# Decode attention on Trainium2: K's words sorted by pairs of heads, dense exponentials, and a mask on the transposed probabilities

## The chip, the cores and the metric

The kernel runs on one core of one Trainium2 chip. The metric is the device time of one execution in microseconds. Three runs of the kernel before took 481.1, 480.31 and 480.0 us; their median is 480.31 us. A profile of one further execution goes with them.

## The reference, cut to what matters

One decode step of a transformer layer for a batch of B = 4 sequences with one new token each, model width D = 576. All inputs are bf16.

```
q = layernorm(x) @ wq                       # 32 query heads of 128
k, v = the last 4096 positions of the caches  # 16 KV heads, 2 query heads on each
p = softmax(q . k / sqrt(128))              # per query head, over 4096 positions
h = x + (p . v) @ wo
out = h + (relu(g) * u) @ W_down            # g, u = layernorm(h) @ W_gate, W_up
```

The caches have 16384 positions, of which the last 4096 are read: 67 MB of K and 67 MB of V. The weights add 25 MB.

## The kernel before, in words

All programs are written out by hand, one per engine. `Sched` (line 51) turns names into semaphore waits: an operation lists the names it depends on, each engine runs its own list strictly in the order written, and all transfers are issued by SP in one list (line 270), each waiting until its place in the SBUF tile `pool` is free.

**Quads and batches.** The 64 pairs of a sequence and a KV head are worked on four heads at a time. A quad is one sequence's four KV heads: 4 MB of K and 4 MB of V. There are 16 quads, and two of them form a batch; there are eight batches, n = 0 to 7. `pool` has four slots of one quad each. In the queue a K quad is followed by the V quad of two quads before, and each waits for the earlier user of its slot: K for its transposes (`("TR", 2i+1)`), V for its matmuls (`("PV", i)`). The weights of the output projection and of the MLP come behind, in the same places.

**Layout of K.** A quad lies in SBUF with partition 4p+s holding head s of 32 position groups p (128 positions t per partition). VectorE transposes it in 32x32 blocks of 4-byte words (`tr`, line 403): a word is two neighbouring features e = 0, 1, and 64 words c, k make a position. One transpose instruction does a quarter of a quad, 2048 words per partition. After it the partition is the word of the feature and the 32 columns of a block are the 32 source partitions, eight position groups k by four heads s. Before the change the output pattern sorts these by head: all columns of head 0, then of head 1 and so on, so that the next written word is 1024 words (4 KB) on. Two instructions fill one of the two buffers of `kT`, which is one block f of the work; there are 32 blocks, four per batch.

**QK** (`qk`, line 540). A block takes 16 matmuls: four heads s by four parts (c, e) of the feature. Each moves 512 columns (64 t by 8 k) through weights `qz`, which are q with zeros elsewhere, and all add into one PSUM bank. The words of a head are contiguous, but of each word a matmul reads one half, so the moving operand has a step of 4 bytes. Row 32g+8r+2s+h of the scores is position group quadrant g, quad r of the batch, head s, query h.

**Softmax** (`rmax`, `fbias`, `trp`, from line 414). Per batch VectorE takes the row maximum, GpSimd makes it common to all rows of a head (`partition_all_reduce`, line 298), and VectorE forms the bias. A V quad lies in SBUF as a K quad does, so after transposing the probabilities partition 4p+s meets head s of V, and there the probabilities of other heads must be zero. Before the change ScalarE makes that so (line 348): it takes the exponential of each score bank four times, u = 0 to 3, with a bias that is about -1.5e38 on rows of other heads than u, and writes copy u to every fourth place of `P`, 8 bytes apart. Two transposes per batch (line 431) then turn `P` into `pT`, 2048 elements per partition each.

**PV** (`pv`, line 556). 32 matmuls per quad move V (512 columns) through weights of 32 columns of `pT`.

**Orders around the change.** TensorE (line 580): blocks 2i and 2i+1 of QK, then PV of quad i-2; so within a batch: QK, QK, PV, QK, QK, PV. At three places `ext` (line 569) stands in front of a PV; it takes finished outputs out. VectorE (line 445): the four transposes of quad 2n, those of quad 2n+1, then `rmax`, `fbias`, `trp` and the row sums of batch n; `norm` (line 439) stands at three places between the two quads and waits for `ext`. A transpose of block f waits until QK of block f-2 has read its buffer. ScalarE: the copies of q into `qz` (`qzero`, line 315), then the batch's exponentials, which wait for the bias, and before the change for the transposes of P of the batch before, since `P` has one buffer.

**Ends.** Before the first batch the layer norm, the q projection (line 523) and its copies (449, 450) run while the first K quad lands. After the last batch come its two PVs, `ext`, `norm`, a shuffle of the outputs (465, 469), the output projection (line 594), the second layer norm and the MLP; W_gate is released by the first of the last PVs, W_up by the second, W_down by the end of the output projection.

Of the kernel before, what the change touches and what calls it, by code (L numbers as in the profile page):

```python
# [6 lines left out]
ACT = mybir.ActivationFunctionType  # L7
ALU = mybir.AluOpType
# [14 lines left out]
NS = 4  # L23
# [80 lines left out]
def bass_sequential_preLN__sliding_block_cached__glu_gated_reglu__decode_kernel(  # L104
# [12 lines left out]
    with ExitStack() as es:  # L117
# [26 lines left out]
        mask = sb("mask", [128, 3, NHB], FP32)  # L144
        selT = sb("selT", [128, 4, H], FP32)
        rmx = sb("rmx", [128, 2], FP32)
        rsel = sb("rsel", [128, NS], FP32)
        bmin = sb("bmin", [128, 2], FP32)
        pmax = sb("pmax", [128, 2, NHB], FP32)
        bcm = sb("bcm", [128, 2, NHB], FP32)  # L150
        t8 = sb("t8", [128, NHB], FP32)
        bias = sb("bias", [128, 2, NS], FP32)
        rs2 = sb("rs2", [128, 2, 2 * NS], FP32)
# [14 lines left out]
        hh = P[:, NG * JW:NG * JW + NG * JW // 2].bitcast(BF16).rearrange("p (g j f) -> p g j f", g=NG, j=JJ)  # L168
        hhT = probT[:, 0, 0:FC * 16].bitcast(BF16).rearrange("p (f b) -> p f b", b=32)
        S8 = probT[:, 0, FC * 16:FC * 16 + 512].bitcast(BF16)  # L170
        Pb = P[:, :].bitcast(BF16).rearrange("p (x s) -> p x s", s=NS)
        Pw = P[:, :].bitcast(BF16)
        x_f = P[0:B, 0:D]
        junk_f = P[0:B, D:2 * D]
        pT = [probT[:, a, :].bitcast(BF16).rearrange("p (a t h) -> p t a h", t=TQ, h=NHQ) for a in range(2)]
# [126 lines left out]
        def prog_act(S):  # L302
            a = "scalar"
            S.dma(a, lambda e: e.dma_start(out=x_bf[:, :], in_=A_x.rearrange("b s d -> (b s) d")), "x", name=land("x"))
            S.op(a, lambda e: e.activation(out=x_f[:, :], in_=x_bf[:, :], func=ACT.Identity, accum_out=st1[:, 0:1]),
                 deps=[land("x")], name="A_SUM")
            S.op(a, lambda e: e.activation(out=junk_f[:, :], in_=x_bf[:, :], func=ACT.Square, accum_out=st1[:, 1:2]),
                 name="A_SQ")
            S.op(a, lambda e: e.activation(out=st1[:, 4:5], in_=st1[:, 3:4], func=ACT.Sqrt, bias=eps_c[0:B, 0:1], scale=1.0),
                 deps=["D_VARC", "EPS"], name="A_STD")  # L310
            S.op(a, lambda e: e.activation(out=xn_bf[:, :], in_=x_f[:, :], func=ACT.Identity,  # L311
                                           bias=st1[:, 6:7], scale=st1[:, 5:6]),
                 deps=["D_NMR", "A_SUM"], name="A_XN")
# [13 lines left out]

            def cpy(b):
                deps = [("PV", NPB * b + NPB - 1)]
                if b >= 2:  # L330
                    deps.append(("EXT", b - 2))
                S.op(a, lambda e: e.copy(out=cp[:, b % 2, :], in_=pb[PVB + b % 2]), deps=deps, name=("CP", b))  # L332

            for i in range(NB):
                qzero(i)
            for n in range(NBATCH):
                for i in range(NB * (n + 1), min(NB * (n + 2), NQUAD)):
                    qzero(i)
                for th in range(2):
                    for u in range(NS):  # L340
                        deps = []
                        if th == 0 and u == 0:
                            deps = [("BIAS", n)]
                            if n >= 1:
                                deps.append(("TRP", n - 1, 1))
                            if n >= 2:
                                deps.append(("RSUM", n - 2))
                        S.op(a, lambda e, n=n, th=th, u=u: e.activation(  # L348
                            out=Pb[:, th * 512:(th + 1) * 512, u], in_=pb[2 * (n % 2) + th], func=ACT.Exp,
                            scale=SCALE, bias=bias[:, n % 2, u:u + 1], accum_out=rs2[:, n % 2, NS * th + u:NS * th + u + 1]),  # L350
                            deps=deps, name=("EXP", n, th) if u == NS - 1 else None, signal=u == NS - 1)
                if n >= 2 and n % 2 == 0:
                    cpy(n // 2 - 1)
            cpy(B - 1)
            S.op(a, lambda e: e.activation(out=st2[:, 24:28], in_=st2[:, 20:24], func=ACT.Sqrt),
                 deps=["D_VARC2"], name="A_STD2")
            for x in PARTS[2:] + PARTS[:2]:
                S.op(a, lambda e, x=x: e.activation(out=gate_sb[:, x[0], :, x[1]:x[2]].rearrange("p j f -> p f j"), in_=part(0, x, "f j"), func=ACT.Relu),
                     deps=[("GATE", x[3])], name=("RELU", x[0], x[1]))
            S.op(a, lambda e: e.copy(out=out_sb[:, 0:HD], in_=pb[DNB][0:B, 0:HD]), deps=["DOWN1"], name="OUT0")  # L360


        def prog_dve(S):
# [24 lines left out]
            for u in range(NS):  # L388
                S.op(v, lambda e, u=u: e.tensor_reduce(out=rsel[:, u:u + 1], in_=mask[:, 1, :].rearrange("p (r s h) -> p s r h", s=NS, h=2)[:, u, :, :],
                                                       axis=AX.XY, op=ALU.max), deps=["M1"] if u == 0 else [], name=f"RSEL{u}")  # L390
# [12 lines left out]
            def tr(i, j):  # L403
                f = 2 * i + j // 2
                deps = [land(("K", i))]
                if f >= NKH:
                    deps.append(("QK", f - NKH))
                x0 = at[("K", i)] + j * (QUAD // 4)
                src = pool[:, x0:x0 + QUAD // 4].bitcast(FP32).rearrange("p (t c k) -> p c t k", c=2, k=32)
                dst = kT[:, f % NKH, :].rearrange("p (s c t k) -> p c t k s", s=NS, c=2, k=8)[:, :, (j % 2) * (TQ // 4):(j % 2 + 1) * (TQ // 4), :, :]  # L410
                src = src.rearrange("p c t (k s) -> p c t k s", s=NS)
                S.op(v, lambda e: e.transpose(out=dst, in_=src), deps=deps, name=("TR", f) if j % 2 else None)  # L412

            def rmax(n):
# [5 lines left out]
            def fbias(n):  # L420
# [4 lines left out]
                S.op(v, lambda e: e.tensor_scalar(out=bias[:, n % 2, :], in0=rsel[:, :], scalar1=bmin[:, n % 2:n % 2 + 1], scalar2=None, op0=ALU.min),  # L425
                     deps=[("BMIN", n), f"RSEL{NS - 1}"] + ([("EXP", n - 2, 1)] if n >= 2 else []), name=("BIAS", n))

            def trp(n):
                for th in range(2):
                    h0, h1 = th * TQ // 2, (th + 1) * TQ // 2  # L430
                    S.op(v, lambda e, h0=h0, h1=h1: e.transpose(out=pT[n % 2][:, h0:h1, :, :], in_=Pw[:, h0 * 32:h1 * 32].rearrange("p (t a h) -> p t a h", a=4, h=NHQ)),  # L431
                         deps=[("EXP", n, th)] + ([("PV", NB * (n - 2) + NB - 1)] if n >= 2 and th == 0 else []), name=("TRP", n, th))
                b, q = divmod(n, 2)
                S.op(v, lambda e: e.tensor_reduce(out=rs1[:, n % 2:n % 2 + 1], in_=rs2[:, n % 2, :], axis=AX.X, op=ALU.add),  # L434
                     name=("RS1", n))
# [72 lines left out]
        def prog_pe(S):  # L508
# [31 lines left out]
            def qk(f):  # L540
                i, th = divmod(f, 2)
                n, r = divmod(i, NB)
                kv_ = kT[:, f % NKH, :].bitcast(BF16).rearrange("p (s c x e) -> p s c e x", s=NS, c=2, e=2)
                deps = [("TR", f)]
                if th == 0:
                    deps.append(("QZ", i))
# [149 lines left out]
```

## Time and profile before

| | |
|---|---|
| runs | 481.1, 480.31, 480.0 us |
| profiled execution, its own time | 481.18 us |
| its span, first to last instruction | 479.9 us |
| busy: TensorE matmul | 283.4 us (59%) |
| busy: VectorE | 301.4 us (63%) |
| busy: ScalarE | 103.8 us (22%) |
| transfers | 159.84 MB, mean 333 GB/s |
| mean granted TensorE clock | 0.839 of full |
| chain that ended last: VectorE, TensorE, ScalarE, DMA | 45%, 27%, 16%, 8% of the span |

A row of the costliest groups gives the line, the engine, the operation, out<-in by the program's names with partitions x elements and type, the count, then busy time and the mean of one in ns, then the idle time of the engine just before, with what ended most of it. All matmuls but the first transposes have line 512, that of a helper, and are told apart by their tiles: `sc<-kT,qz` is QK, `pb<-pool,probT` with 512 columns is PV. DVE is VectorE, ACT ScalarE, PE TensorE, POOL GpSimd. The chain of work that ended last lists start, duration and what ran; "issue" is time in which the engine waited for nothing that the profile shows. The timeline lists the same columns for all instructions of an engine, neighbours merged with a count.

### The profile page before, as it was taken

To read this page: it belongs to the slowest core of one execution; us is meant where nothing else is said; L and a number is where in the kernel's file an instruction comes from. 1 tells how busy PE (TensorE), PEld (TensorE's weight loads), DVE (VectorE), ACT (ScalarE), POOL (GpSimd) and SP (SyncE) were. 2 spreads that over 40 slices of the span, in tenths; PEclk is the share of its full clock that TensorE was granted. 3 is DMA by queue.
4 is the path that set the end of the run, shared out by engine and by line. 5 is a ranking of instruction groups with operands and counts; after the bars stand their busy time and mean duration, and the time that the engine had idled before them with its cause. 6 is when DMAs were issued, how large, how long until landed. Compare 5 with 4: busy or idle time off the path is not lost.

```text
span 479.9 us, 3896 instructions
## 1 busy us (share of the span) xinstructions
PE 283.4 (59%) x1669; PEld 127.4 (27%) x1684; DVE 301.4 (63%) x201; ACT 103.8 (22%) x213; POOL 8.2 (2%) x22
## 2 busy tenths in 40 slices
PE   0326702994299429690599069742894286939575
PEld 0312200341034114230243024211341142314553
DVE  0289639963996395917992778539963959140313
ACT  3010090008000800043005300080008000441002
POOL 3100000000000000000000000000000000000000
PEclk9999865898599859996799679895999599879569
DMA  8999990599859986898199948994689768926996
GB/s 347 429 436 437 436 402 8 216 393 436 355 219 393 436 352 262 350 419 369 44 385 427 421 167 350 433 393 180 262 359 438 341 262 350 384 99 237 422 409 265
DMA packets 7377, 159.84 MB, mean 333 GB/s; under 512 B 824, under 2 KB 960, under 8 KB 2112
## 3 DMA queue, kind: packets, MB, share of 16 engines
q1 hardware_dynamic: 7352, 159.59, 79.6%
q8 instruction: 13, 0.21, 0.2%
q14 instruction: 4, 0.03, 0.0%
q10 hardware_dynamic: 8, 0.00, 0.0%
HBM read 159.58 MB, written 0.00 MB: 333 GB/s over the span
## 4 chain that ended last, share of the span: by engine, by line
DVE 45%; PE 27%; ACT 16%; DMA 8%; issue 1%; SPq 1%; POOL 1%
DVE kT L412 35%; PE sc L512 17%; ACT P L348 16%; PE pb L512 10%; DMA pool<-in_A_k_cache_dram 5%; DVE probT L431 4%; DMA pool<-in_B_W_down_dram 3%; DVE rmx L415 2%; SPq L259 1%; POOL bcm L298 1%; DVE P L469 0%; DVE pmax L417 0%; DVE bias L425 0%; DVE rowsum L436 0%; DVE t L421 0%
## 5 line engine op out<-in xcount | busy, mean ns | idle before, releaser
L412 DVE STREAM_TRANSPOSE kT<-pool 128x2048 f32<-128x2048 f32 x64 | 229.3, 3704 | 3.6 <-DMA pool<-in_A_k_cache_dram 3.6
L512 PE MATMUL sc<-kT,qz 128*128 128x512 bf16 x497 | 138.0, 437 | 150.6 <-DVE kT L412 149.9
L512 PE MATMUL pb<-pool,probT 128*32 128x512 bf16 (+1 forms) x584 | 119.8, 372 | 10.9 <-DVE rs L434 7.8
L512 PEld LDWEIGHTS sc<-kT,qz 128*128 128x128 bf16 x512 | 52.0, 107 | 236.1 <-DVE kT L412 161.2
L348 ACT ACTIVATE P<-sc,bias 128x512 bf16<-128x512 f32 x64 | 77.5, 1417 | 55.7 <-DVE bias L425 55.7
L431 DVE STREAM_TRANSPOSE probT<-P 128x2048 bf16<-128x2048 bf16 x16 | 37.0, 2312 | 59.6 <-ACT P L348 59.6
L512 PEld LDWEIGHTS pb<-pool,probT 128*32 128x32 bf16 (+1 forms) x584 | 51.3, 96 | 77.6 <-issue 9.1
L325 ACT COPY qz<-qrep 32x32 bf16<-32x32 bf16 x64 | 13.9, 218 | 255.4 <-PE sc L512 244.2
L415 DVE TENSOR_REDUCE rmx<-sc 128x1 f32<-128x1024 f32 x8 | 9.8, 1224 | 35.6 <-PE sc L512 35.6
L440 DVE RECIPROCAL rs_sb<-pb 128x32 f32<-128x32 f32 x4 | 1.4, 358 | 30.7 <-PE pb L512 30.7
L348 ACT ACTIVATION_READ_ACCUMULATOR P<-sc,bias 128x1 f32 x64 | 18.8, 295 | 0.0
L519 PE MATMUL pb<-ident_b,xn_bf 4*128 4x4 bf16 (+1 forms) x5 | 0.4, 180 | 19.7 <-ACT xn_bf L311 19.7
L298 POOL PARTITION_ALL_REDUCE bcm<-pmax x8 | 3.1, 388 | 394.0 <-DVE pmax L417 394.0
L512 PE MATMUL sc<-oX,pool 128*128 128x4 bf16 (+1 forms) x160 | 6.8, 177 | 5.0 <-DVE oX L472 3.7
L373 DVE COPY sel<-ident_b 128x128 bf16<-128x128 bf16 x4 | 1.1, 450 | 11.8 <-POOL ident_b L283 11.8
L512 PEld LDWEIGHTS sc<-oX,pool 128*128 128x128 bf16 (+1 forms) x160 | 6.6, 123 | 5.4 <-issue 5.3
L332 ACT COPY cp<-pb 128x512 f32<-128x512 f32 x4 | 2.7, 673 | 17.6 <-PE pb L512 17.6
L512 PE MATMUL sc<-pool,hnT 128*32 128x288 bf16 (+2 forms) x112 | 5.8, 328 | 0.0
L499 DVE TENSOR_TENSOR P<-pb,P 128x288 bf16<-128x288 f32 (+1 forms) x2 | 0.8, 402 | 7.7 <-PE sc L512 7.7
L519 PEld LDWEIGHTS pb<-ident_b,xn_bf 4*128 4x128 bf16 (+1 forms) x5 | 0.3, 117 | 19.7 <-ACT xn_bf L311 19.7
L474 DVE TENSOR_TENSOR R_sb<-sc,xT 128x16 f32<-128x16 f32 x1 | 0.2, 174 | 8.3 <-PE sc L512 8.3
L512 PEld LDWEIGHTS pb<-selT,cp 128*128 128x128 f32 x32 | 4.1, 191 | 1.7 <-ACT cp L332 1.2
(103 smaller groups left out, 75.1 us busy)
## 6 DMA issues: line engine op xcount, KB each, us to landing
pool<-in_A_k_cache_dram SPq DMA_DIRECT2D x16, 4096.0 KB, 17.8
pool<-in_A_v_cache_dram SPq DMA_DIRECT2D x16, 4096.0 KB, 13.9
pool<-in_A_wo_dram SPq DMA_DIRECT2D x4, 1152.0 KB, 9.7
pool<-in_B_W_gate_dram SPq DMA_DIRECT2D x1, 4608.0 KB, 13.6
pool<-in_B_W_up_dram SPq DMA_DIRECT2D x1, 4608.0 KB, 20.1
pool<-in_A_wq_dram SPq DMA_DIRECT2D x1, 4096.0 KB, 13.2
pool<-in_B_W_down_dram SPq DMA_DIRECT2D x2, 1296.0 KB, 11.7
pool<-in_B_W_down_dram SPq DMA_DIRECT2D x5, 432.0 KB, 14.8
```

What stands on the lines that cost most here:

```text
L259: lambda e, g0=g0, g1=g1, j0=j0, nj=nj: e.dma_start(out=wd_sb[:, g0:g1, j0 * D:(j0 + nj) * D], in_=B_W_down[g0 * 128 * JJ:g1 * 128 * JJ, : ...
L298: S.op(g, lambda e, n=n: e.partition_all_reduce(bcm[:, n % 2, :], pmax[:, n % 2, :], 128, bass_isa.ReduceOp.max), deps=deps, name=("PAR", n))
L325: S.op(a, lambda e, src=src, dst=dst: e.copy(out=dst, in_=src), deps=deps, name=("QZ", i) if g == 3 else None, signal=g == 3)
L332: S.op(a, lambda e: e.copy(out=cp[:, b % 2, :], in_=pb[PVB + b % 2]), deps=deps, name=("CP", b))
L348: S.op(a, lambda e, n=n, th=th, u=u: e.activation(out=Pb[:, th * 512:(th + 1) * 512, u], in_=pb[2 * (n % 2) + th], func=ACT.Exp, scale=SCA ...
L373: S.op(v, lambda e, ce=ce: e.tensor_copy(out=sel[:, ce, :, :], in_=bass.AP(tensor=ident_b, offset=64 * (ce // 2) + ce % 2, ap=[[128, 128], ...
L412: S.op(v, lambda e: e.transpose(out=dst, in_=src), deps=deps, name=("TR", f) if j % 2 else None)
L415: S.op(v, lambda e: e.tensor_reduce(out=rmx[:, n % 2:n % 2 + 1], in_=sc[:, (n % 2) * 1024:(n % 2 + 1) * 1024], axis=AX.X, op=ALU.max), dep ...
L431: S.op(v, lambda e, h0=h0, h1=h1: e.transpose(out=pT[n % 2][:, h0:h1, :, :], in_=Pw[:, h0 * 32:h1 * 32].rearrange("p (t a h) -> p t a h", ...
L440: S.op(v, lambda e: e.reciprocal(out=rs_sb[:, b, :], in_=pb[OB][:, 64 + b * H:64 + (b + 1) * H]), deps=[("SUM", b)], name=("RS", b))
L499: S.op(v, lambda e, x=x: e.tensor_tensor(out=hh[:, x[0], :, x[1]:x[2]], in0=part(1, x, "j f"), in1=gate_sb[:, x[0], :, x[1]:x[2]], op=ALU. ...
L512: S.op(t, lambda e: e.matmul(o, lhsT=l, rhs=r, start=start, stop=stop, skip_group_check=skip), deps=deps, name=name, signal=name is not None)
```

## The change

It has four parts. (1) The transposes of K sort the 32 columns of a block by pairs of heads only: the output pattern runs over position group x, pair a and head within the pair s, so two neighbouring words (8 bytes) are written together, and the next two 8 KB on. (2) QK reads its head out of such a pair: the moving operand has a step of 8 bytes in runs of eight columns, 128 bytes apart. (3) ScalarE takes each exponential once, with one bias column, and writes it densely; `P` becomes double-buffered, so the exponentials wait for the transposes of two batches before. The transposes of P read each element four times over (a step of 0), which puts a copy on the partitions of all four heads. (4) VectorE then multiplies `pT` of each of the two quads by a mask `m8` (one where the partition's head is the row's, zero elsewhere), in place, 1024 elements per partition; PV waits for that product. Three small operations of the set-up are replaced by three others (`RSEL`, `M4`, `M8`).

```diff
-        rsel = sb("rsel", [128, NS], FP32)
+        rsel = sb("rsel", [128, 1], FP32)
+        m4 = sb("m4", [128, NS], FP32)
+        m8 = sb("m8", [128, NS, 2], BF16)
...
-        Pb = P[:, :].bitcast(BF16).rearrange("p (x s) -> p x s", s=NS)
-        Pw = P[:, :].bitcast(BF16)
+        Pb = P[:, :].bitcast(BF16)
...
-                    for u in range(NS):
-                        deps = []
-                        if th == 0 and u == 0:
-                            deps = [("BIAS", n)]
-                            if n >= 1:
-                                deps.append(("TRP", n - 1, 1))
-                            if n >= 2:
-                                deps.append(("RSUM", n - 2))
-                        S.op(a, lambda e, n=n, th=th, u=u: e.activation(
-                            out=Pb[:, th * 512:(th + 1) * 512, u], in_=pb[2 * (n % 2) + th], func=ACT.Exp,
-                            scale=SCALE, bias=bias[:, n % 2, u:u + 1], accum_out=rs2[:, n % 2, NS * th + u:NS * th + u + 1]),
-                            deps=deps, name=("EXP", n, th) if u == NS - 1 else None, signal=u == NS - 1)
+                    deps = []
+                    if th == 0:
+                        deps = [("BIAS", n)]
+                        if n >= 2:
+                            deps += [("TRP", n - 2, 1), ("RSUM", n - 2)]
+                    x0 = (n % 2) * 1024 + th * 512
+                    S.op(a, lambda e, n=n, th=th, x0=x0: e.activation(
+                        out=Pb[:, x0:x0 + 512], in_=pb[2 * (n % 2) + th], func=ACT.Exp,
+                        scale=SCALE, bias=bias[:, n % 2:n % 2 + 1], accum_out=rs2[:, n % 2, th:th + 1]),
+                        deps=deps, name=("EXP", n, th))
...
+            S.op(v, lambda e: e.tensor_reduce(out=rsel[:, :], in_=mask[:, 1, :], axis=AX.X, op=ALU.max), deps=["M1"], name="RSEL")
+            S.op(v, lambda e: e.tensor_reduce(out=m4[:, :], in_=ident_b[:, :].rearrange("p (b s) -> p s b", s=NS), axis=AX.X, op=ALU.add), name="M4")
+            S.op(v, lambda e: e.tensor_copy(out=m8[:, :, :], in_=bass.AP(tensor=m4, offset=0, ap=[[NS, 128], [1, NS], [0, 2]])), deps=["M4"], name="M8")
...
-                src = pool[:, x0:x0 + QUAD // 4].bitcast(FP32).rearrange("p (t c k) -> p c t k", c=2, k=32)
-                dst = kT[:, f % NKH, :].rearrange("p (s c t k) -> p c t k s", s=NS, c=2, k=8)[:, :, (j % 2) * (TQ // 4):(j % 2 + 1) * (TQ // 4), :, :]
-                src = src.rearrange("p c t (k s) -> p c t k s", s=NS)
+                src = pool[:, x0:x0 + QUAD // 4].bitcast(FP32).rearrange("p (x a s) -> p x a s", a=2, s=2)
+                dst = kT[:, f % NKH, :].rearrange("p (a x s) -> p x a s", a=2, s=2)[:, (j % 2) * TQ * 4:(j % 2 + 1) * TQ * 4, :, :]
...
-                S.op(v, lambda e: e.tensor_scalar(out=bias[:, n % 2, :], in0=rsel[:, :], scalar1=bmin[:, n % 2:n % 2 + 1], scalar2=None, op0=ALU.min),
+                S.op(v, lambda e: e.tensor_tensor(out=bias[:, n % 2:n % 2 + 1], in0=rsel[:, :], in1=bmin[:, n % 2:n % 2 + 1], op=ALU.min),
...
+                    src = bass.AP(tensor=P, offset=((n % 2) * 1024 + th * 512) // 2, ap=[[TQ * 16, 128], [1, 256]]).bitcast(BF16)
+                    src = bass.AP(tensor=src.tensor, offset=src.offset, ap=[src.ap[0], [1, 512], [0, NS]])
+                    dst = pT[n % 2][:, h0:h1, :, :]
+                    S.op(v, lambda e, src=src, dst=dst: e.transpose(out=dst, in_=src),
...
+                for a in range(NB):
+                    w = pT[n % 2][:, :, a, :]
+                    S.op(v, lambda e, w=w: e.tensor_tensor(out=w, in0=w, in1=bass.AP(tensor=m8, offset=0, ap=[[NHQ, 128], [0, TQ], [1, NHQ]]), op=ALU.mult),
+                         deps=[("TRP", n, 1)] + (["M8"] if n == 0 else []), name=("W", n, a))
...
-                kv_ = kT[:, f % NKH, :].bitcast(BF16).rearrange("p (s c x e) -> p s c e x", s=NS, c=2, e=2)
+                kv_ = kT[:, f % NKH, :].bitcast(BF16).rearrange("p (a t c k s e) -> p a s c e t k", a=2, c=2, k=8, s=2, e=2)
...
-                        mm(pb[2 * (n % 2) + th], qz[:, r, s, ce, :], kv_[:, s, ce // 2, ce % 2, :],
+                        mm(pb[2 * (n % 2) + th].rearrange("p (t k) -> p t k", k=8), qz[:, r, s, ce, :], kv_[:, s // 2, s % 2, ce // 2, ce % 2, :, :],
...
-                deps = [("TRP", n, 1), land(("V", i))]
+                deps = [("W", n, a), land(("V", i))]
```

More of the change, by code (lines that the diff above doesn't have):

```diff
@@ L151, in bass_sequential_preLN__sliding_block_cached__glu_gated_reglu__decode_kernel @@
         t8 = sb("t8", [128, NHB], FP32)
-        bias = sb("bias", [128, 2, NS], FP32)
-        rs2 = sb("rs2", [128, 2, 2 * NS], FP32)
+        bias = sb("bias", [128, 2], FP32)
+        rs2 = sb("rs2", [128, 2, 2], FP32)
         rs1 = sb("rs1", [128, 2], FP32)
@@ L387, in prog_dve @@
             S.op(v, lambda e: e.tensor_reduce(out=mask8[:, :], in_=ident_b[:, :].rearrange("p (s k) -> p s k", s=8), axis=AX.X, op=ALU.add), name="MASK8")
-            for u in range(NS):
-                S.op(v, lambda e, u=u: e.tensor_reduce(out=rsel[:, u:u + 1], in_=mask[:, 1, :].rearrange("p (r s h) -> p s r h", s=NS, h=2)[:, u, :, :],
-                                                       axis=AX.XY, op=ALU.max), deps=["M1"] if u == 0 else [], name=f"RSEL{u}")
+            S.op(v, lambda e: e.tensor_reduce(out=rsel[:, :], in_=mask[:, 1, :], axis=AX.X, op=ALU.max), deps=["M1"], name="RSEL")
+            S.op(v, lambda e: e.tensor_reduce(out=m4[:, :], in_=ident_b[:, :].rearrange("p (b s) -> p s b", s=NS), axis=AX.X, op=ALU.add), name="M4")
+            S.op(v, lambda e: e.tensor_copy(out=m8[:, :, :], in_=bass.AP(tensor=m4, offset=0, ap=[[NS, 128], [1, NS], [0, 2]])), deps=["M4"], name="M8")
             S.op(v, lambda e: e.reciprocal(out=st1[:, 5:6], in_=st1[:, 4:5]), deps=["A_STD"], name="D5")
@@ L424, in fbias @@
                      deps=[("T8", n)], name=("BMIN", n))
-                S.op(v, lambda e: e.tensor_scalar(out=bias[:, n % 2, :], in0=rsel[:, :], scalar1=bmin[:, n % 2:n % 2 + 1], scalar2=None, op0=ALU.min),
-                     deps=[("BMIN", n), f"RSEL{NS - 1}"] + ([("EXP", n - 2, 1)] if n >= 2 else []), name=("BIAS", n))
+                S.op(v, lambda e: e.tensor_tensor(out=bias[:, n % 2:n % 2 + 1], in0=rsel[:, :], in1=bmin[:, n % 2:n % 2 + 1], op=ALU.min),
+                     deps=[("BMIN", n), "RSEL"] + ([("EXP", n - 2, 1)] if n >= 2 else []), name=("BIAS", n))
             def trp(n):
@@ L430, in trp @@
                     h0, h1 = th * TQ // 2, (th + 1) * TQ // 2
-                    S.op(v, lambda e, h0=h0, h1=h1: e.transpose(out=pT[n % 2][:, h0:h1, :, :], in_=Pw[:, h0 * 32:h1 * 32].rearrange("p (t a h) -> p t a h", a=4, h=NHQ)),
+                    src = bass.AP(tensor=P, offset=((n % 2) * 1024 + th * 512) // 2, ap=[[TQ * 16, 128], [1, 256]]).bitcast(BF16)
+                    src = bass.AP(tensor=src.tensor, offset=src.offset, ap=[src.ap[0], [1, 512], [0, NS]])
+                    dst = pT[n % 2][:, h0:h1, :, :]
+                    S.op(v, lambda e, src=src, dst=dst: e.transpose(out=dst, in_=src),
                          deps=[("EXP", n, th)] + ([("PV", NB * (n - 2) + NB - 1)] if n >= 2 and th == 0 else []), name=("TRP", n, th))
+                for a in range(NB):
+                    w = pT[n % 2][:, :, a, :]
+                    S.op(v, lambda e, w=w: e.tensor_tensor(out=w, in0=w, in1=bass.AP(tensor=m8, offset=0, ap=[[NHQ, 128], [0, TQ], [1, NHQ]]), op=ALU.mult),
+                         deps=[("TRP", n, 1)] + (["M8"] if n == 0 else []), name=("W", n, a))
                 b, q = divmod(n, 2)
```

## The prediction

> **What bounds the kernel now.** I read four views, in this order. First the page's costliest groups, for what one instruction of each kind takes:
>
> ```profile
> L412 DVE STREAM_TRANSPOSE kT<-pool 128x2048 f32<-128x2048 f32 x64 | 229.3, 3704 | 3.6 <-DMA pool<-in_A_k_cache_dram 3.6
> L512 PE MATMUL sc<-kT,qz 128*128 128x512 bf16 x497 | 138.0, 437 | 150.6 <-DVE kT L412 149.9
> ...
> L348 ACT ACTIVATE P<-sc,bias 128x512 bf16<-128x512 f32 x64 | 77.5, 1417 | 55.7 <-DVE bias L425 55.7
> L431 DVE STREAM_TRANSPOSE probT<-P 128x2048 bf16<-128x2048 bf16 x16 | 37.0, 2312 | 59.6 <-ACT P L348 59.6
> ```
>
> Two transposes of 2048 elements differ by 1.4 us, and VectorE (DVE) idles 59.6 us for the exponentials: both things that the change attacks. Second, the chain of work that ended last, in order of time, for one batch (start us, us, what):
>
> ```profile
> 223.35 14.21 DVE kT L412 x4
> 237.56 0.05 issue
> 237.60 3.79 PE sc L512 x16
> 241.40 7.01 PE pb L512 x32
> 248.41 0.17 issue
> 248.58 7.20 PE sc L512 x31
> 255.80 1.24 DVE rmx L415
> ...
> 258.49 9.70 ACT P L348 x16
> 268.21 2.31 DVE probT L431
> ...
> 270.60 0.23 DVE rowsum L436
> ```
>
> A batch is one loop: K transposes (the first four are the start), then TensorE finishes its four blocks of 16 QK matmuls with a PV of 32 in between, then maximum, bias, exponentials, transposes of P, and the next batch. It is 47.5 us here and 54 us where norm() sits in it; the seven batches from 74.1 to 427.4 average 50.5. The queue of transfers is not the bound: a batch needs 4 x 4.19 MB, 38.5 us at the 436 GB/s of the page's best slices. Third, TensorE alone in the timeline:
>
> ```profile
> 237.60 3.79 PE L512 MATMUL sc<-kT,qz 128*128 128x512 bf16 x16 [2.04 <-DVE kT L412]
> 241.33 7.08 PE L512 MATMUL pb<-pool,probT 128*32 128x512 bf16 x32
> ```
>
> One QK matmul lasts 388 ns and one PV 379 in these windows, so the steps are (3790-388)/15 = 227 ns and (7080-379)/31 = 216 ns, at full clock. PV reads V densely, QK reads K at 4-byte steps. Fourth, the groups by shape, for what reading far apart costs:
>
> ```profile
> L469 DVE TENSOR_REDUCE P<-P 128x128 f32<-128x1024 f32 x1 | 2.0, 1966 | 0.0
> ...
> L465 DVE TENSOR_TENSOR P<-sc,mask 128x1024 f32<-128x1024 f32 x1 | 1.2, 1225 | 1.1 <-PE sc L512 1.1
> ...
> L461 DVE COPY probT<-ident_b 128x1024 bf16<-128x1024 bf16 x1 | 1.1, 1060 | 0.0
> ```
>
> L465 (1225 ns, 1024 dense elements) and L450 (691 ns, 512) give 1.04 ns an element and 157 ns fixed. L469 reads one word every 16 bytes: (1966-157)/1024 = 1.77 ns each. L461 also steps by 16 bytes, and at two elements at a time it is (1060-157)/512 = 1.76 ns. And the QK step is 227 ns for 512 columns at 4 bytes, 128 pieces of 16 bytes: 1.77 ns each. Three rows on two engines give one number, so I read it as the time of one 16-byte piece from SBUF, and the QK matmul as already at that limit, just above its dense 216.
>
> **The change, part by part.** Times are from S, where a batch's first K transpose starts.
>
> K transposes. Before, every written word lies 4 KB from the last: 1.72 ns each ((3704-179)/2048; the 179 ns fixed from L431 and L502, 479 ns for 288). After, words are written in pairs of 8 bytes. If a place costs 1.72 ns, a pair has 2.08 ns of element time over it, and nothing is left: 2312 ns, as L431 with its 16-byte runs. Ends: 2312 and 3704; I take 2312. Successive starts are some 0.16 us closer than one lasts (3.55 against 3.70), so 2.15. QK may then start at 2.15+2.31+0.04 = S+4.5 instead of S+7.2.
>
> QK matmuls. Same number, but a head's columns now lie 8 bytes apart, two per 16-byte piece: 256 pieces, 256 x 1.77 = 453 ns. The low clock no longer matters to them (427 ns now). Ends: 216 (no limit) and 512 x 1.77 = 906 (a piece per element); taken 453, from the nearest row, QK itself. All 64 now lie end to end, since transposes take 4.3 us a block and matmuls 7.25: 64 x 0.453 = 29.0, plus the PV between (7.0) and waits and drain (0.45): last score at 4.5+29.0+7.0+0.45 = S+40.9. Now it is 255.80-223.26 = S+32.5. **This gives back 8.4 us a batch.**
>
> [...]
>
> Maximum to exponential: 255.80 to 258.49, 2.7 us, kept (the bias is one column instead of four).
>
> Exponentials. The first transpose of P now waits for one instead of four: 0.85 us instead of 5.0. L307 (576 dense elements with an accumulator) takes 0.76 from its start to the end of its accumulator read; the first L348 as it is now, with its read, takes 1.4. Ends 0.75 and 1.4; a little above the dense row. The second exponential ends under the first transpose of P. That transpose reads each element four times over but makes as many elements: 2.15+2.31 = 4.46 for both.
>
> Masks W: two products of 1024 16-bit elements per batch. No row shows one; ends 0.69 (two elements at a time, as L461: 157 + 512 x 1.04) and 1.23 (L465). I take 0.69, because L461 is the row with 16-bit data in SBUF, spaced 0.6; the two and the row sums' 0.3 make 1.5. [...] PV waits for W; behind W on DVE stand the row sum and the next K transposes, which TensorE waits for, so W is on the path.
>
> So last score to next S is 2.7+0.85+4.46+1.5 = 9.5 (now 14.9), and **a batch is 40.9+9.5 = 50.4 us**. In three of them ext() stands in TensorE's order, 1.4 us (186.81 to 188.16); norm() on DVE then falls where TensorE is behind anyway, while today it costs 6.8. Seven batches: 7 x 50.4 + 3 x 1.4 = 357.
>
> The first batch: the first transpose at 24.99 is set by K's landing and stays. q's copies take 1.7 us as now, the second transpose ends at 31.1, four blocks of 7.25 end at 60.3 (now 59.1), and 9.5 later S is 69.9 (now 74.1). So the last batch ends at 69.9+357 = 427 (now 427.4).
>
> The tail: the first of the two last PVs starts after its own W, 0.8 before the batch's end (now 0.3). TensorE will have idled only 2 us, so the ten matmuls at 427 ns that open it now run at 216: 2.1 saved. From there transfers set the end (W_gate is released at 436.25, at that PV's end). Together 2.6 earlier, so the span is 479.9-2.6 = 477.3.
>
> Costed at nothing: the extra mask set-up (M4, M8, less three RSEL), some 0.3 us before q is normalised, hidden by 2 us between q's last matmul (24.9) and the end of the first K transpose (27.1); uncovered it is 0.3. SP's queue: K's slots are freed at the same places of the loop, and 38.5 us of transfers fit into 50.
>
> The profiled execution took 481.18 with a span of 479.9; the median of the runs is 480.31, 0.4 over that span. On the median's scale: 477.3+0.4 = **477.7 us**. 0.2% (1 us) is what a measurement here can tell.
>
> **Rivals.**
> 1. No limit at 8 bytes, two columns to a piece hide it: QK at 216 to 227 ns. Last score at about S+28 (TensorE opens at the low clock after 7 us idle), 37.9 with the 9.5; then the 38.5 us of transfers bind with some slack: 39 a batch, 57+7x39+50 = 380 us. For: weight loads at 8-byte steps, in the output projection, come 136 in 5.61 us, 41 ns per 128 columns. Against: the three rows at 1.77.
> 2. The other side: pairs do not merge, and the K transpose keeps half or all of its surcharge. Its place is the opening two transposes, the only ones in front of TensorE: half, 3.0 us, adds 1.4 x 8 = 11, **489 us**; all, 500. It decides from 2.5 us on. For: L348 writes 2-byte elements 8 bytes apart and pays about 1.18 us for 512, as if nothing merged. Against: there no two touch, here each pair does.
> 3. W at one element at a time: 16 x 0.53 = 8.5, 486 us.
> 4. The clock: QK limited by reads moves columns in 48% of full-clock cycles; if that counts as idle, the PV on the path opens at 427: 2 to 7 us a batch, 495 to 530. Against: from 417.6 to 421.0 TensorE was busy 1.72 of 3.40 us, and the granted clock was 1.00 there and in the 3.3 us after it.
> 5. Each element its own piece: 906 ns, 64 x 0.453 x 8 = 232 more, 710 us.
> 6. The exponential isn't shorter written densely: 1.4 instead of 0.85, 482 us.
>
> **How the numbers follow.** Forecast 0.50 (its own range 471 to 484: 5 ns on the QK step are 2.6 us), rivals 0.10, 0.13, 0.12, 0.08, 0.04, 0.03. The forecast is so near to no change that 0.35 of its 0.50 falls to faster, 0.08 to same, 0.07 to slower. Faster: 0.35+0.10 = 0.45. Same: 0.08, and 0.02 of the sixth: 0.10. Slower: the rest, 0.45. The range 466 to 505 takes in the forecast, rivals 2, 3, 6 and half of 4, some 0.82; it leaves out 380 and everything above.
>
> **What would show it.** Right: QK steps of about 450 ns at both clocks; K transposes at 2.3 us; W at 0.7; TensorE as releaser of the K transposes and the chain's largest share; batches of 50 us. Wrong: QK steps near 220 (then DMA near 9 tenths throughout and 380 us), K transposes over 2.5, PV opening at 427 ns inside a batch.

## The result and the profile after

| | before | after |
|---|---|---|
| median of four runs each | 480.15 us (479.62 to 481.1) | 486.75 us (486.12 to 487.51) |
| ratio | | 1.0136, 95% interval 1.0114 to 1.0158 |
| profiled execution, its own time | 481.18 us | 486.12 us |
| its span | 479.9 us | 484.8 us |
| mean granted TensorE clock | 0.839 | 0.916 |
| busy: TensorE matmul, VectorE, ScalarE | 283, 301, 104 us | 387, 224, 38 us |

The change made the kernel 1.4% slower. The forecast was 477.7 us, 9.05 us too low and on the other side of no change (faster); the range of 466 to 505 held the time.

First the costliest groups of the page of after, for the four instructions that the change touches and the new one (mean ns is the second number behind the bar):

```profile
L517 PE MATMUL sc<-kT,qz 128*128 128x512 bf16 x512 | 244.3, 652 | 59.8 <-DVE kT L410 59.8
L410 DVE STREAM_TRANSPOSE kT<-pool 128x2048 f32<-128x2048 f32 x64 | 142.9, 2284 | 36.1 <-PE sc L517 32.4
...
L432 DVE STREAM_TRANSPOSE probT<-P 128x2048 bf16<-128x2048 bf16 x16 | 36.0, 2290 | 6.8 <-ACT P L347 6.8
...
L347 ACT ACTIVATE P<-sc,bias 128x512 bf16<-128x512 f32 x16 | 10.8, 682 | 58.4 <-DVE bias L423 58.4
L436 DVE TENSOR_TENSOR probT<-probT,m 128x1024 bf16<-128x1024 bf16 x16 | 10.3, 688 | 0.3
```

Read the releasers at the ends of the lines. The transposes of P waited 59.6 us for ScalarE and now wait 6.8. The transposes of K, which waited for no other engine, now wait 32.4 us for TensorE: they are 1.4 us shorter each, and of the pair of K transposes and QK they are now the faster. Second, the shares of the chain that ended last, by engine and by line:

```profile
PE 66%; DVE 22%; DMA 8%; ACT 1%; SPq 1%; issue 1%; POOL 1%
```

Before it was 45% VectorE, 27% TensorE, 16% ScalarE. Third, the same chain in order of time for one batch (start, duration, what; it is the batch that answers to the one from 223.35 shown of before):

```profile
226.84 4.42 DVE kT L410 x2
231.25 0.05 issue
231.30 15.28 PE sc L517 x32
246.58 7.01 PE pb L517 x32
253.59 15.23 PE sc L517 x32
268.84 1.24 DVE rmx L413
...
271.46 0.79 ACT P L347 x2
272.27 4.52 DVE probT L432 x2
276.81 1.29 DVE probT L436 x2
...
278.44 4.42 DVE kT L410 x2
```

The batch takes 278.44 - 226.84 = 51.6 us, against 47.5. The part behind the last score shrank from 15.0 to 9.6 us (268.84 to 278.44), as the change means it to. The part before it, from the first K transpose to the last score, grew from 32.5 to 42.0 us, and TensorE works without a gap from 231.30 to 268.84. (These are the chain's figures. The prediction counts from the transpose's own start in the timeline, which is 0.09 us earlier, here 226.75; so it has 14.9 us for before.) Fourth, TensorE's timeline, for the step of a QK matmul (the first batch's 64 and a later batch's 32):

```profile
30.91 30.40 PE L517 MATMUL sc<-kT,qz 128*128 128x512 bf16 x64 [3.14 <-DVE kT L410]
...
75.46 15.28 PE L517 MATMUL sc<-kT,qz 128*128 128x512 bf16 x32 [14.15 <-DVE kT L410]
```

The 32 further matmuls of the first line take 30.40 - 15.28 = 15.12 us, so the step is **472 ns**, where it was 227 and the prediction had 453.

Where the time went, between the two profiled executions, by the timeline: first batch, from the start to the second batch's first transpose, 74.1 to 70.9 us (-3.2); seven batches 353.2 to 364.3 (+11.1), although the three batches with ext() and norm() are now 1.0 us longer than the others, where it was about 7; from there to the end 52.6 to 49.6 (-3.0). Together +4.9, the difference of the spans.

### The profile page after: what moved, and what is told of

The parts are those of the page before. It is cut to its first block, busy times and chain, and to the rows that moved or that the text cites. A ratio compares the mean times of both kernels' runs of the same rounds, so it can differ in the third digit from the quotient of the medians.

```text
span 484.8 us, 3831 instructions
## 1 busy us (share of the span) xinstructions
PE 386.8 (80%) x1684; PEld 133.6 (28%) x1684; DVE 224.3 (46%) x216; ACT 38.3 (8%) x117; POOL 8.2 (2%) x22
## 4 chain that ended last, share of the span: by engine, by line
PE 66%; DVE 22%; DMA 8%; ACT 1%; SPq 1%; issue 1%; POOL 1%
PE sc L517 52%; PE pb L517 14%; DVE probT L432 7%; DVE kT L410 7%; DMA pool<-in_A_k_cache_dram 5%; DMA pool<-in_B_W_down_dram 3%; DVE rmx L413 2%; DVE probT L436 2%; ACT P L347 1%; SPq L260 1%; POOL bcm L299 1%; DVE P L474 0%; DVE pmax L415 0%; DVE rowsum L441 0%; DVE t L419 0%
## 5 line engine op out<-in xcount | busy, mean ns | idle before, releaser
L517 PE MATMUL sc<-kT,qz 128*128 128x512 bf16 x512 | 244.3, 652 | 59.8 <-DVE kT L410 59.8
L410 DVE STREAM_TRANSPOSE kT<-pool 128x2048 f32<-128x2048 f32 x64 | 142.9, 2284 | 36.1 <-PE sc L517 32.4
L517 PEld LDWEIGHTS sc<-kT,qz 128*128 128x128 bf16 x512 | 59.2, 118 | 237.1 <-issue 173.1
L517 PE MATMUL pb<-pool,probT 128*32 128x512 bf16 (+1 forms) x584 | 117.9, 368 | 5.6 <-DMA pool<-in_B_W_down_dram 2.7
L432 DVE STREAM_TRANSPOSE probT<-P 128x2048 bf16<-128x2048 bf16 x16 | 36.0, 2290 | 6.8 <-ACT P L347 6.8
L347 ACT ACTIVATE P<-sc,bias 128x512 bf16<-128x512 f32 x16 | 10.8, 682 | 58.4 <-DVE bias L423 58.4
L436 DVE TENSOR_TENSOR probT<-probT,m 128x1024 bf16<-128x1024 bf16 x16 | 10.3, 688 | 0.3
L372 DVE COPY sel<-ident_b 128x128 bf16<-128x128 bf16 x4 | 1.1, 449 | 11.1 <-POOL ident_b L284 11.1
L517 PE MATMUL pb<-selT,cp 128*128 128x32 f32 x32 | 4.1, 270 | 0.7 <-ACT cp L333 0.7
```

Source lines behind the costliest of these rows:

```text
L347: S.op(a, lambda e, n=n, th=th, x0=x0: e.activation(out=Pb[:, x0:x0 + 512], in_=pb[2 * (n % 2) + th], func=ACT.Exp, scale=SCALE, bias=bias ...
L372: S.op(v, lambda e, ce=ce: e.tensor_copy(out=sel[:, ce, :, :], in_=bass.AP(tensor=ident_b, offset=64 * (ce // 2) + ce % 2, ap=[[128, 128], ...
L432: S.op(v, lambda e, src=src, dst=dst: e.transpose(out=dst, in_=src), deps=[("EXP", n, th)] + ([("PV", NB * (n - 2) + NB - 1)] if n >= 2 an ...
L436: S.op(v, lambda e, w=w: e.tensor_tensor(out=w, in0=w, in1=bass.AP(tensor=m8, offset=0, ap=[[NHQ, 128], [0, TQ], [1, NHQ]]), op=ALU.mult), ...
L517: S.op(t, lambda e: e.matmul(o, lhsT=l, rhs=r, start=start, stop=stop, skip_group_check=skip), deps=deps, name=name, signal=name is not None)
```

## The experiments

Each kernel's time is compared with the kernel before run on the same chip (479.45 to 480.3 us). A step is the median distance of two QK matmuls' starts in the trace; a run has 512 of them, and some traces hold 497. "Piece" means 16 bytes of SBUF on every partition, as in the prediction.

**1. The softmax half alone.** The K transposes and the QK reads of before, everything else of the change:

```diff
-                dst = kT[:, f % NKH, :].rearrange("p (a x s) -> p x a s", a=2, s=2)[:, (j % 2) * TQ * 4:(j % 2 + 1) * TQ * 4, :, :]
+                dst = kT[:, f % NKH, :].rearrange("p (s c t k) -> p c t k s", s=NS, c=2, k=8)[:, :, (j % 2) * (TQ // 4):(j % 2 + 1) * (TQ // 4), :, :]
...
-                kv_ = kT[:, f % NKH, :].bitcast(BF16).rearrange("p (a t c k s e) -> p a s c e t k", a=2, c=2, k=8, s=2, e=2)
+                kv_ = kT[:, f % NKH, :].bitcast(BF16).rearrange("p (s c x e) -> p s c e x", s=NS, c=2, e=2)
```

> The K transposes and the QK reads of before (words of a head contiguous, 4-byte step), with the changed softmax (dense exponentials, spread transposes, mask). Theory: the softmax half of the change gains 5.4 us a batch (14.9 to 9.5 us from last score to the next K transpose) and the K half loses it again. Then a batch is 32.5 + 9.5 = 42.0 us, 48.8 with norm, the first ends at 68.6, and the whole is 68.6 + 4 x 42.0 + 3 x 48.8 + 50 + 0.4 = about 433 us. Rival: the softmax half gains little in the old setting because transfers (38.5 us a batch) or the old chain take its place: 460 to 480 us.

Measured: **436.5 us** (four runs, 434.62 to 438.19), ratio 0.9076 (0.9039 to 0.9112). From the page of this kernel:

```profile
DVE 55%; PE 30%; DMA 9%; ACT 2%; issue 1%; SPq 1%; POOL 1%
...
L411 DVE STREAM_TRANSPOSE kT<-pool 128x2048 f32<-128x2048 f32 x64 | 229.5, 3722 | 3.4 <-DMA pool<-in_A_k_cache_dram 3.4
L518 PE MATMUL sc<-kT,qz 128*128 128x512 bf16 x512 | 144.7, 444 | 107.7 <-DVE kT L411 107.7
...
L347 ACT ACTIVATE P<-sc,bias 128x512 bf16<-128x512 f32 x16 | 10.8, 682 | 55.8 <-DVE bias L424 55.8
```

The K transposes wait only for the first K quad's transfer (3.4 us) and never for TensorE, and TensorE waits 107.7 us for them: the K transposes bound, as in before, and the 4 x 1.4 us a batch that they are longer cost less than the QK of after. This is the version that beats both kernels, by 9.2% and, against the 486.75 of after, by 10%.

**2. The K half alone.** The kernel before with the new transposes of K and the new QK reads, and the old softmax (the two edits of experiment 1 the other way round).

> The changed K transposes and QK reads alone, with the softmax of before (four exponentials per bank, 14.9 us from last score to the next K transpose instead of 9.5). Theory: parts add, so 486.8 + 8 x 5.4 = 530 us. Rival: TensorE's longer work hides the longer softmax: nearer 490.

Measured: 532.1 us (one run), step 472 ns. From its page, first the chain, then the groups:

```profile
PE 60%; DVE 15%; ACT 15%; DMA 7%; SPq 1%; issue 1%; POOL 1%
...
L511 PE MATMUL sc<-kT,qz 128*128 128x512 bf16 x512 | 244.3, 652 | 97.9 <-DVE kT L411 97.9
...
L348 ACT ACTIVATE P<-sc,bias 128x512 bf16<-128x512 f32 x64 | 77.5, 1417 | 59.2 <-DVE bias L424 59.2
```

The QK line is that of after to the nanosecond, and the exponentials are those of before. So the change is two edits of opposite sign: softmax 480.3 to 436.5, -43.8 us; K 479.8 to 532.1, +52.3 us. They add to +8.5, and together measured +6.6; where the 2 us between come from was not tested.

**3. The same step, no jumps.** After reads runs of eight columns at 8 bytes (64 bytes) and then skips 64 bytes. Here 512 columns follow each other at 8 bytes:

```diff
-                        mm(pb[2 * (n % 2) + th].rearrange("p (t k) -> p t k", k=8), qz[:, r, s, ce, :], kv_[:, s // 2, s % 2, ce // 2, ce % 2, :, :],
+                        o = (s // 2) * 4096 + (ce // 2) * 2048 + (s % 2) * 2 + ce % 2
+                        mm(pb[2 * (n % 2) + th], qz[:, r, s, ce, :], kv_[:, o:o + 2045:4],
```

> The changed kernel, but each QK matmul reads 512 columns at an even 8-byte step, without the 64 jumps between runs of 8 columns (it reads other words, so the scores are not the reference's). Theory A (each 16-byte piece costs 1.845 ns): the step stays 472 ns and the time 487 us. Theory B (a piece costs 1.77 ns, and each of the 64 jumps 0.3 ns more): 453 ns and 477 us. No piece limit at all: near 216 to 227.

Measured: 476.32 us (one run), span 475.0. Its timeline of TensorE:

```profile
31.20 29.10 PE L517 MATMUL sc<-kT,qz 128*128 128x512 bf16 x64 [3.14 <-DVE kT L410]
...
74.45 14.63 PE L517 MATMUL sc<-kT,qz 128*128 128x512 bf16 x32 [14.15 <-DVE kT L410]
```

(29.10 - 14.63)/32 = 452 ns. Nothing but the read pattern differs from after, and the span is 9.8 us shorter; 512 matmuls at 20 ns less are 10.2. The prediction's 453 ns were the price of this pattern and not of the one in the change.

**4. What the price hangs on.** Seven more patterns, each with the read of after exchanged and nothing else, to find whether a jump costs, or the 8-byte step, or the place of the pieces. These kernels, like that of experiment 3, read other words than the scores need, so only their times count. The edits are other rearrangements of `kv_`, for instance 64 runs of eight columns at 4 bytes, and 128 runs of four at 8 bytes:

```diff
-                kv_ = kT[:, f % NKH, :].bitcast(BF16).rearrange("p (a t c k s e) -> p a s c e t k", a=2, c=2, k=8, s=2, e=2)
+                kv_ = kT[:, f % NKH, :].bitcast(BF16).rearrange("p (a t c s k e) -> p a s c e t k", a=2, c=2, k=8, s=2, e=2)
...
+                        mm(pb[2 * (n % 2) + th].rearrange("p (t k) -> p t k", k=4), qz[:, r, s, ce, :], kv_.rearrange("p (t c k s e) -> p c s e t k", c=4, k=4, s=2, e=2)[:, s, ce // 2, ce % 2, :, :],
```

> The changed kernel, but each QK matmul reads 64 runs of 8 columns at a 4-byte step, with a jump of 128 bytes from run to run (other words, so the scores are not the reference's). Theory A (price per piece only): 128 pieces, 227 to 236 ns. Theory B (0.3 ns a jump): 227 + 19 = 246 ns. In both, TensorE no longer sets the batch, and the time falls to 380 to 390 us, since the K transposes stay at 2.3 us.

> The changed kernel, but each QK matmul reads 32 runs of 16 columns at a 4-byte step (64 bytes a run, then 64 bytes skipped; other words, so the scores are not the reference's). Runs of 8 (32 bytes, then 96 skipped) gave 216 ns, an even 4-byte step 227. Theory C (16-byte pieces cost more when they follow each other without a gap in long runs): between, near 227. Theory D (runs of 64 bytes with 64 skipped use half the places that could serve, and cost more, as 472 against 452 at 8 bytes): 235 to 240 ns.

> The changed kernel, but each QK matmul reads 128 runs of 4 columns at an 8-byte step (32 bytes a run, then 96 skipped; other words, so the scores are not the reference's). Theory B (0.3 ns a jump): 128 jumps, 452 + 40 = 492 ns. Theory C (the gap behind 32 bytes helps, as at 4 bytes): at or below 452 ns.

> The changed kernel, but each QK matmul reads 512 columns at an even 16-byte step (other words, so the scores are not the reference's). If 16 bytes are the piece, each column is its own: 512 x 1.77 = 905 ns a matmul, and the time is 476 + 512 x 0.453 = 708 us. If the limit has another size of piece (32 bytes, or a rate that saturates), the step stays near 452 to 500 ns.

> The changed kernel, but each QK matmul reads 512 neighbouring 2-byte columns (other words, so the scores are not the reference's). Theory (reading sets the 227 ns of the kernel before): 216 ns, as PV. Rival (the 128-column weights cost the 11 ns): 227 ns. The time is 380 to 385 us in both.

> The changed kernel, but each QK matmul reads 128 runs of 4 columns at an 8-byte step, 32 bytes a run and then 32 skipped (other words, so the scores are not the reference's). Theory E (a gap behind every two pieces brings the price from 1.77 down to 1.68 ns): 430 ns, 465 us. Theory F (what counts is how evenly the 64-byte places of a 128-byte stretch are used): 452 ns, 476 us. Theory B (0.3 ns a jump): 490 ns.

> The changed kernel, but each QK matmul reads 32 runs of 16 columns at an 8-byte step, 128 bytes a run and then 128 skipped (other words, so the scores are not the reference's). Theory B (0.3 ns a jump): 452 + 10 = 462 ns, 481 us. Theory F: 452 ns, 476 us. Any half-used stretch costs as much as 64 of 128 bytes: 472 ns, 487 us.

Measured, with the kernels above (one run each, but for after; of before, with its other softmax, only the step is listed; ns per piece is the step over the pieces of a matmul):

| columns lie | run, then skipped | pieces | step, ns | ns per piece | time, us |
|---|---|---|---|---|---|
| dense | - | 64 | 216 | - | 381.35 |
| 4 bytes apart (before) | flat | 128 | 227 | 1.77 | - |
| 4 bytes apart | 32, 96 bytes | 128 | 216 | 1.69 or less | 384.06 |
| 4 bytes apart | 64, 64 bytes | 128 | 235 | 1.84 | 381.67 |
| 8 bytes apart | flat | 256 | 452 | 1.77 | 476.32 |
| 8 bytes apart | 32, 96 bytes | 256 | 431 | 1.68 | 465.2 |
| 8 bytes apart | 32, 32 bytes | 256 | 430 | 1.68 | 464.8 |
| 8 bytes apart (after) | 64, 64 bytes | 256 | 472 | 1.84 | 486.75 |
| 8 bytes apart | 128, 128 bytes | 256 | 430 | 1.68 | 465.89 |
| 16 bytes apart | flat | 512 | 900 | 1.76 | 722.51 |

Two lines of the timeline carry the last row but one of the table; they are of the kernel with 128-byte runs, and (27.79 - 13.98)/32 = 432 ns, the mean where the table has the median:

```profile
31.43 27.79 PE L517 MATMUL sc<-kT,qz 128*128 128x512 bf16 x64 [3.14 <-DVE kT L410]
73.37 13.98 PE L517 MATMUL sc<-kT,qz 128*128 128x512 bf16 x32 [14.15 <-DVE kT L410]
```

What follows. The number of pieces sets the step: flat reads of 128, 256 and 512 pieces give 1.77, 1.77 and 1.76 ns. That a piece has 16 bytes is the prediction's reading. Pieces of 8 bytes are out (they would make the flat steps of 8 and 16 bytes cost the same, and they cost 452 and 900 ns), but every strided QK read here covers whole stretches of 32 bytes, so pieces of 32 bytes at twice the price would fit as well. A price on each jump is out: it would have made 128 runs cost 492 ns, and they cost 431, less than no jumps at all; that theory B had the right number in experiment 3 was luck. The 8-byte step as such is out too: the pattern of 64 bytes read and 64 skipped costs 1.84 ns a piece at 4 bytes as at 8. What moves the price by 4 to 5% either way is where the pieces lie: 64 of 128 bytes is dear, 32 of 64, 32 of 128 and 128 of 256 are cheap, and flat is between. Why that is so stays open; none of the theories had the 430 ns of the 128-byte runs or the 216 ns of runs of eight at 4 bytes. Nor does VectorE's traffic explain the 472 ns: in the batch above VectorE is busy 8.84 of the 15.30 us from 231.30 on and idle from 253.60 to 268.80, and TensorE's 32 matmuls take 15.28 and 15.23 us.

The three fastest are bound elsewhere. From the page of one of them, with runs of eight at 4 bytes:

```profile
DMA packets 7376, 159.83 MB, mean 418 GB/s; under 512 B 824, under 2 KB 960, under 8 KB 2112
...
q1 hardware_dynamic: 7352, 159.59, 97.7%
```

The transfers are busy 97.7% of the span, and 98.3% in the other two: about 380 us is the floor that the prediction's first rival named, reached as soon as QK leaves the limit.

**5. Both halves without the 8-byte read, first try.** If a quad lands so that a head's eight position groups lie on neighbouring partitions, one K transpose writes runs of eight words and QK reads at 4 bytes. For that each quad comes in four transfers of 32 partitions (the mask, the spreading read of `P` and the QK read are made to fit):

```diff
-            return cache[b, NS * m:NS * m + NS, SK - WIN:SK, :].rearrange("s (p t) d -> p s (t d)", p=32)
+            w0 = SK - WIN + g * (WIN // 4)
+            return cache[b, NS * m:NS * m + NS, w0:w0 + WIN // 4, :].rearrange("s (k t) d -> s k (t d)", k=8)
```

> A layout that has neither price: each quad is loaded by four transfers of 32 partitions, so that a quadrant's partitions are sorted by head and then position group; the transposes of K then write runs of 8 words and QK reads contiguous words at a 4-byte step. Softmax as changed. Theory (QK bound by 16-byte pieces, K transposes by scattered words): K transposes 2.3 us, QK steps 227 ns, last score about 28 us after a batch's first transpose, 38 us a batch with the softmax, and the 38.5 us of transfers bind: about 380 us, DMA near 9 tenths. Rival: transfers of 32 partitions reach only part of the rate and set the time: at half the rate 134 MB alone take 615 us, about 660 us in all.

Measured: 1331.9 us. The slices of the transfers, from its page:

```profile
DMA  5222222222222222222222222222222222245746
GB/s 206 106 110 107 110 106 110 107 110 106 108 108 108 109 107 109 108 109 106 110 107 109 108 107 109 108 109 107 109 107 109 107 108 108 109 137 152 178 174 278
```

A mean busy share of two to three tenths with 107 GB/s, against nine tenths with 430 before: the rate fell to a quarter, and the busy share about as far. The pattern in DRAM now begins with s, of size 4, where it began with 32 position groups, and each transfer fills 32 partitions instead of 128. No run varied one of these alone, so which of them sets the rate is not shown; nor does a mean share tell a few busy engines from all of them busy for part of the time. The compute side did what was wanted, 2280 ns for a K transpose and a QK step of 227 ns, but it cannot be had in this way.

**6. Second try.** Two transfers a quad, each to every second partition, with 16 position groups outermost; the K transposes write pairs of words of one head.

```diff
-            return cache[b, NS * m:NS * m + NS, SK - WIN:SK, :].rearrange("s (p t) d -> p s (t d)", p=32)
+            return cache[b, NS * m:NS * m + NS, SK - WIN:SK, :].rearrange("s (x u t) d -> u x s (t d)", x=16, u=2)[u]
```

> Two transfers of 64 partitions each per quad (every second partition) put two position groups of one head side by side; then the K transposes write pairs of 8 bytes that belong to one head, each head's words lie contiguous, and QK reads at a 4-byte step as before. Softmax as changed. Theory: K transposes 2.3 us as in the changed kernel, QK steps 227 ns as in the kernel before, batches bound by the 38.5 us of transfers: 380 to 390 us, transfers near 420 GB/s in the mean. Rival: transfers to every second partition are slower, and the time lies between that and 1330 us (what the load by 32 partitions gave).

Measured: 658.17 to 675.61 us (four runs). From the page of the shortest:

```profile
DMA  9999999999999999999999999999999999999996
GB/s 342 209 216 220 217 208 214 218 219 210 223 223 221 224 231 223 223 228 231 231 227 243 228 231 237 237 238 239 239 245 242 236 235 239 248 245 253 438 412 282
```

Here the transfers are busy throughout (99.2% of the 16 engines' span) and move half as much: 210 to 250 GB/s, and 438 again once the weights come to all 128 partitions. What halves the rate was not tested. K transposes of 2282 ns and the step of 227 ns show once more that the compute side is not at fault.

## Why the prediction was wrong, point by point

**The failed step is "256 pieces, 256 x 1.77 = 453 ns".** The count of 256 pieces was right, and so was what was made of it: the QK step goes with the pieces (452 ns for 256 read flat, 900 for 512), and TensorE becomes the bound (66% of the chain). The price was taken from a flat read and used for a read that takes 64 bytes and skips 64: it measured 1.84 ns, 472 instead of 453; a flat read at 8 bytes did measure 452 (experiment 3). At 512 matmuls, all on the path, 19 ns are 9.7 us, more than the 7.5 us by which the span was missed. Why this pattern costs 4% more than a flat one stays open. "5 ns on the QK step are 2.6 us" was the prediction's own warning. Its range for the step's forecast case, 471 to 484 us, did not allow for a price that moves by 4%, and the forecast was 0.5% from no change.

**The other terms, by the sum's own order.**

- K transposes 2312 ns, measured 2284, no longer than the transposes of P (L432, 2290): rival 2 did not happen. QK starts at S+4.55 (predicted 4.5).
- Last score S+42.1 (predicted 40.9). 4.55 + 64 x 0.472 + 7.0 + 0.3 gives it; the 1.2 are the failed step.
- Maximum to exponential 2.6 us (2.7). Exponential to first transpose 0.81 (0.85): 682 ns written densely against 1417 spread; rival 6 did not happen.
- Transposes of P 4.52 for both (4.46). W 688 ns each, 1.29 for two (0.69 each; 1.5 with the row sums), the end that the prediction took; rival 3 did not happen.
- Last score to the next S: 9.5 (9.5). Batch 51.6 (50.4); ext adds 1.0 in three (1.4).
- The second batch's S = 70.9 (69.9): 1.2 by the failed step again, less a start of QK 0.2 earlier (30.91).
- Tail: the two last PVs 13.15 us against 15.17, 2.0 saved (2.1).

From the last batch's end on, 49.6 us passed, 0.8 less than in the sum. About half of that is a slip of the sum itself: its own terms for the end (the last batch over 0.4 earlier, the PV 0.5 earlier against that, 2.1 saved in it) make 3.0 us, and it counted 2.6.

**The balance.** First batch +1.0, seven batches 364.3 instead of 357, +7.3, tail -0.8: the span is 484.8 instead of 477.3, 7.5 more. By terms that is +9.7 for the read and -2.2 for ext (1.0 instead of 1.4, three times), the tail and small change; had these come as predicted, the miss would have been larger. The other 1.5 us of the miss are no work at all: the prediction put the median 0.4 us above the span, as the profiled run of before was 0.9 above the median of its runs; that of after is the shortest of its four (486.12; median 486.75, 1.95 over the span).

**The rivals.** Rival 1, no limit at 8 bytes, did not happen: two columns to a 16-byte piece cost 430 to 472 ns where dense reads cost 216. Half of rival 1 stands: 380 us is what the kernel takes when QK is near 216 to 235. Rival 5 (906 ns, 710 us) is what a 16-byte step comes to, 900 ns and 722.5 us, and not an 8-byte step. Rival 4, the clock, did not happen at 472 ns, but at 900 ns it did. Granted clock is the number behind the engines' busy times (PE first) in these stretches of one batch; first after, QK opening, QK, and the PV that follows:

```profile
231.30:238.30 7.00, 7.00 (x15) 1.89 (x16) 4.33 (x2) 0.00 (x0) 0.00 (x0) 0.58 0.85 337
238.30:246.50 8.20, 8.20 (x18) 1.88 (x16) 4.51 (x2) 0.00 (x0) 0.00 (x0) 1.00 1.04 448
246.60:250.00 3.40, 3.40 (x17) 1.50 (x18) 3.38 (x2) 0.87 (x4) 0.00 (x0) 1.00 0.00 0
```

Then the kernel with the 16-byte step, the end of a QK stretch, the PV behind it (two rows) and the opening of the next QK stretch:

```profile
527.00:541.00 14.00, 14.00 (x16) 1.74 (x14) 4.40 (x2) 0.00 (x0) 0.00 (x0) 0.50 0.13 56
541.20:546.00 4.80, 4.80 (x12) 1.68 (x13) 4.51 (x2) 0.88 (x4) 0.00 (x0) 0.52 0.00 0
546.00:550.50 4.50, 4.50 (x21) 1.90 (x21) 0.00 (x0) 0.00 (x0) 0.00 (x0) 1.00 0.00 0
551.40:560.00 8.60, 8.60 (x10) 1.15 (x10) 0.00 (x0) 0.00 (x0) 0.00 (x0) 0.77 0.97 408
```

PE is busy throughout in all of them. A QK matmul of after moves its columns at 216/472 = 46% of the dense rate, and the clock rose to 1.00 within the stretch and stayed there. At 216/900 = 24% it was 0.50 at the end of one stretch, so that the PV opened at half speed (12 matmuls in 4.80 us). It stood at 1.00 at the end of the PV and fell again in the next stretch (0.77 in the mean), although PE was never idle in these 8.60 us. No run has a QK rate between 24% and 46%. The QK steps did not change with the clock: 472 ns at 0.58 as at 1.00.

**What the expected gain turned into.** In the two chains of one batch, before's and after's, the part behind the last score gives 5.4 us. In front of it the K transposes give 9.8 (14.2 to 4.4), but QK, which stood on the path with 3.79 + 7.20 = 11.0 us and ran beside the transposes otherwise, stands on it with 15.28 + 15.23 = 30.5, 19.5 more. The net is a batch 4.1 us longer; the shorter transposes only wait (32.4 us for TensorE).

## What to carry to other kernels

TensorE's strided operand cost 1.68 to 1.84 ns here for each 16-byte piece that it touched, where that came to more than the dense 216 ns, and a small price on the path times 512 decides a change: take the price from a row with the same runs and gaps, or give it the spread of the rows that there are. A change with two halves should be priced, and if it can be tried, by halves: here one half is worth 9% and the other costs more than that. A layout that suits the compute engines is worth nothing if the transfers that make it run at a quarter or at half of their rate (107 and 210 to 250 GB/s here, against 430).

## What the runs showed of the hardware that was not expected

- The price of a piece for TensorE's moving operand is 1.68, 1.77 or 1.84 ns by where the pieces lie (for the 64-of-128-byte pattern 1.84 at 4- as at 8-byte steps), and the 472 ns of after did not change with the clock (0.58 or 1.00).
- A busy TensorE that moved columns at 24% of the dense rate was held at or brought down to a clock of 0.50; at 46% it was granted 1.00.
- A transpose that writes 4-byte words in neighbouring pairs takes 2284 ns, against 3704 to 3722 with every word apart. ScalarE's exponentials take 1417 ns when their 2-byte results lie 8 bytes apart, against 682 when they lie densely.
- The same 4 MB in four transfers of 32 partitions came at 107 GB/s, in two of every second partition at 210 to 250, in one of 128 at about 430.
